# A gated attention and SwiGLU kernel: value fetches five attention steps later, four more places for transposed terms, and the output projection in float16 terms

## Chip, core and metric

One core of a Trainium2 chip runs the kernel. The core has five engines with instruction queues of their own: TensorE (PE; its weight loads are shown apart as PEld), VectorE (DVE), ScalarE (ACT), GpSimd (POOL) and SyncE (SP), which here issues every DMA. The metric is device microseconds of one execution; lower is better. The time before is the median of three runs.

## What is computed

The reference, cut to what matters (S = 2048 rows, D = 576, 32 heads of 18, 4 segments of 512 rows, F = 4608):

```python
def _A_ref(x, wq, wk, wv, wo, beta):              # attention with a memory
    q, k, v = heads(x @ wq), heads(x @ wk), heads(x @ wv)
    g = sigmoid(beta); M = 0; z = 0
    for s in range(4):
        p = softmax(qs @ ks.T * scale + mask)     # mask: -1e9 where key > query
        a_mem = (phi(qs) @ M) / (phi(qs) @ z + 1e-6)
        outs.append(g * a_mem + (1 - g) * (p @ vs))
        M = M + phi(ks).T @ vs; z = z + phi(ks).sum()
    return concat(outs) @ wo                      # the output projection

def _B_ref(x, w_gate, w_up, w_down):
    return (silu(x @ w_gate) * (x @ w_up)) @ w_down

g = sigmoid((x * gate_w).sum(-1, keepdims=True))
return g * _A_ref(x, ...) + (1 - g) * _B_ref(x, ...)
```

Inputs and outputs are float32. The kernel keeps the precision by splitting each operand of a matmul into a rounded high part and the low rest, and adding the products high x high, high x low and low x high.

## The kernel before

**Stages.** First come the projections to q, k and v and the memory term, segment by segment (`qk`, `v_step`, `upd_gen`, `mem_step`; to about 233 us). Their results go to DRAM: stacked bfloat16 terms of q and k (`stk`, `stw`), of v (`vd`), and the memory's part of the output (`med`). Then a loop over 72 positions works off the feed-forward part, with attention mixed in: `seq` has two halves of 1024 rows with 36 blocks of 128 hidden columns each. The first half also makes the float16 terms of the weights (`w_make`, kept in `wc` for the second half). Last comes the output projection over 16 tiles of 128 rows (`c_load`, `c_tr`, `products`).

**A position.** Gate and up projection of a block are made from seven products (`seven(t, j)`): six matmuls with 512 columns (line 1392) and one with the remainder rows of the weights, the tile `rh` (line 1395), which `r_fetch` loads from `rc` by line 356. After each product comes a beat (`tick`, `beat`), k = 0 to 7. In a beat run, in this order: the functions that were deferred to it (`defer`, a list of queues by beat); down projection groups, as many as `SHARE[k]` says; and steps of the attention. A down group (`down_part`, line 1161) is 9 matmuls of float16 terms into one PSUM bank, with 320 or 256 output columns, from three hidden blocks; DVE then adds the bank into `ya` (`down_end`, lines 1168 and 1170). Every third position 16 new groups are due. At position 3, the first with groups, another table `FSHARE` holds. Between the halves lies the break: ten beats without products, in which the last 16 groups of the first half run (two with `k` 0 and 1, the rest without a `k`).

**Attention.** `att_gen` is a generator, and each `next` is one step `tau`. Five steps make a unit of two heads in one segment (64 units). A step computes scores of the unit at hand (`s_bank`, line 890) for the row maxima. For most units the maximum row goes through DRAM (`m_store`, line 982; `row_load`, line 301) and the scores are computed again transposed twelve steps later (`t_bank`, line 1001), then exp on ACT (1005), a mask on POOL (1013), a split by DVE and POOL (1101, 1105) and the products with v (`pv_step`, 1029 and 1031). In the second half every other unit is turned instead: its exp is split into `pq` (946, 947), and a transposing DMA (`turn`, line 951) writes it to `pk`, from where `pv_turned` (963, 964) reads it. `homes` lists the places: six each for `pq` and `pk`. The table `TURN` says how many steps after the scores each part follows. `v_fetch` (line 306) loads the v terms of four units into one of two buffers. How many steps a beat runs comes from a credit that `TICK` fills; in the first half beats 0 and 1 give none, except in the break, where `brk` lets them.

**Order on the queues.** The schedule is manual: each engine executes its instructions in the order in which the program emits them, so a wait holds back all that follows on that engine. SP holds all DMA issues. In the first half ACT also squares raw weights for the scales of later blocks (`glance`: load by line 1371, square by line 141). `x_second` makes the terms of the second half's input from position 24 on, with low parts on DVE by line 1321.

**Output projection.** `wo_load` splits `wo` into float32r parts (1208, 1209). For each tile `c_tr` adds the memory's part, transposes through PE (1234, 1236), and splits into `oh`, `ol` and `os_` (133, 134). `products` (224) then runs 14 matmuls for each half of 288 columns, and DVE scales by the gate `gg` and adds the feed-forward part (1562, 1563).

## Time and profile before

| | |
|---|---|
| median of 3 runs | 1727.56 us (1726.11 to 1729.72) |
| the profiled execution | 1725.81 us, span 1724.1 us, mean granted clock 0.998 |
| projections and memory | 0 to 233 us |
| first half: positions 0 to 35 | 233 to 903 us |
| break | 903 to 926 us |
| second half: positions 36 to 71 | 926 to 1634 us |
| output projection (with the last down groups) | 1634 to 1724 us |
| busy: PE, DVE, ACT, POOL | 98%, 78%, 62%, 51% of the span |
| DMA | 311 MB, 61.8% of the 16 engines' time in the hardware queue |

How to read it: times count from the span's start. In a group or a timeline row stand line, engine, operation, output <- input with sizes, and in brackets the idle time before it with what ended it. A row of waits has the sum, the count and the longest. A row of the chain of waits has start and length on the path that ended last; matmuls of one run are merged there, so length over count is the pitch, while the duration of one matmul in other rows includes its way through the array. A row of a stretch has its limits, its length, and the busy time of PE, PEld, DVE, ACT and POOL, then the granted clock, DMA share and GB/s.

### The profile page before, as it was taken

The page shows a single profiled execution, that of the slowest core. Times are in us where ns is not written, and L with a number is a line of the kernel's source. Part 1 is how long each engine was busy: PE and PEld are TensorE (multiplying, and loading weights), DVE is VectorE, ACT ScalarE, POOL GpSimd, SP SyncE. Part 2 cuts the span into 40 slices and gives each one's busy share as a digit, 9 for nine tenths or more (in the row PEclk, how much of TensorE's full clock was granted, in tenths as well). Part 3 has the DMA queues.
Part 4 walks back from the last instruction along what each step waited for, and adds up shares of the span by engine and source line. Part 5 has one row for each costly group of instructions (what it writes and reads, how often), then busy time and mean ns, then how long its engine had stood idle before and what let it go on. Part 6 is the DMA issues. An engine that isn't in the chain of part 4 may idle for free.

```text
span 1724.1 us, 35228 instructions
## 1 busy us (share of the span) xinstructions
PE 1684.5 (98%) x12267; PEld 1093.1 (63%) x12267; DVE 1347.3 (78%) x3286; ACT 1066.3 (62%) x1907; POOL 885.6 (51%) x1187
## 2 busy tenths in 40 slices
PE   9999998999999999999999999999999999999999
PEld 7898865556655665565555556656656655665599
DVE  6687666789888988888886888887878787875555
ACT  6666567677777777766774664665565566464411
POOL 3336552266656665565553755555555555543121
PEclk9999999999999999999999999999999999999999
DMA  8666675665776666536435476786587669653543
GB/s 282 219 229 221 221 257 203 206 210 169 239 229 198 184 220 194 171 112 193 158 124 172 118 173 154 164 196 146 132 203 174 129 166 203 155 122 115 183 142 137
DMA packets 341670, 311.30 MB, mean 181 GB/s; under 512 B 193396, under 2 KB 258676, under 8 KB 341492
## 3 DMA queue, kind: packets, MB, share of 16 engines
q1 hardware_dynamic: 341492, 309.05, 61.8%
q8 instruction: 96, 1.57, 0.4%
q14 instruction: 82, 0.67, 0.1%
HBM read 183.20 MB, written 99.55 MB: 164 GB/s over the span
## 4 chain that ended last, share of the span: by engine, by line
PE 71%; DVE 10%; ACT 9%; issue 3%; DMA 3%; POOL 2%; SPq 1%; DVEq 0%; ACTq 0%; POOLq 0%
PE bank L1392 30%; PE bank L1161 19%; PE bank L224 7%; PE bank L1395 5%; PE bank L890 3%; PE bank L1001 2%; PE bank L1029 1%; ACT L1499 1%; DVE ya L1170 1%; ACT row L1499 1%; ACT pe L1005 1%; PE bank L1031 1%; PE bank L963 1%; DVE junk L908 1%; DMA stw<-q 1%
## 5 line engine op out<-in xcount | busy, mean ns | idle before, releaser
L1161 PE MATMUL bank<-dw,hh 128*128 128x320 f16 (+1 forms) x2304 | 437.9, 287 | 13.8 <-DVE ya L1170 9.5
L1161 PE MATMUL bank<-dw,hl 128*128 128x320 f16 (+1 forms) x1152 | 330.5, 287 | 0.9 <-DVE dw L1141 0.6
L1105 POOL TENSOR_TENSOR p<-pe,p 128x512 f16<-128x512 f32 x220 | 271.7, 1235 | 78.7 <-DVE p L1101 50.2
L1161 PEld LDWEIGHTS <-hh 128*128 128x128 f16 x2304 | 224.9, 98 | 100.9 <-issue 19.9
L1005 ACT ACTIVATE pe<-bank 128x512 f32<-128x512 f32 x220 | 130.1, 591 | 190.6 <-PE bank L1001 181.9
L1170 DVE SCALAR_TENSOR_TENSOR ya<-bank,sc,ya 128x320 f32<-128x320 f32 x352 | 177.2, 511 | 57.2 <-PE bank L1161 55.0
L1395 PE MATMUL bank<-xr,rh 128*128 128x512 f16 x504 | 191.2, 379 | 1.9 <-DMA rh<-rc 1.9
L908 DVE CUSTOM_DVE_ANT_0 junk<-bank,cm 128x128 bf16<-128x128 f32 (+2 forms) x352 | 169.3, 481 | 14.0 <-PE bank L890 7.4
L1013 POOL TENSOR_SCALAR_AFFINE_SELECT pe<-pe 128x256 f32<-128x256 f32 (+1 forms) x220 | 89.5, 407 | 164.6 <-ACT pe L1005 153.0
L1264 DVE SCALAR_TENSOR_TENSOR hl<-hh,row 128x512 f16<-128x512 f16 x144 | 125.2, 870 | 47.8 <-ACT hh L1261 46.7
L1161 PEld LDWEIGHTS <-hl 128*128 128x128 f16 x1152 | 112.7, 98 | 30.2 <-DVE hl L1264 0.6
L890 PE MATMUL bank<-kst,qst 108*128 108x512 bf16 (+3 forms) x512 | 124.8, 299 | 5.9 <-ACT pe L1005 5.2
L1001 PE MATMUL bank<-qst,kst 111*128 111x512 bf16 (+3 forms) x352 | 103.3, 300 | 3.9 <-ACT pe L1005 2.8
L1101 DVE CAST p<-pe 128x512 f16<-128x512 f32 x202 | 106.4, 527 | 0.0
L1497 DVE TENSOR_TENSOR row<-bank,row 128x512 f32<-128x512 f32 x72 | 49.7, 690 | 64.4 <-ACT bank L1496 64.4
L370 POOL TENSOR_TENSOR ws<-raw 128x256 f32<-128x256 f32 x72 | 66.5, 924 | 64.2 <-DMA raw<-in_wf_dram 35.3
L224 PE MATMUL bank<-xo,qhi 128*128 128x512 f32 x288 | 93.0, 403 | 0.5 <-DVE xo L134 0.2
L1261 ACT ACTIVATE hh<-row 128x512 f16<-128x512 f32 x144 | 89.0, 618 | 3.8 <-DVE row L1507 3.8
L467 POOL TENSOR_TENSOR q<-qr,q 128x512 bf16<-128x512 f32 x36 | 47.8, 1328 | 84.3 <-ACT q L466 74.8
L1492 ACT ACTIVATE row<-bank 128x512 f32<-128x512 f32 x72 | 42.9, 596 | 76.4 <-PE bank L1395 76.2
L1395 PEld LDWEIGHTS <-rh 128*128 128x128 f16 x504 | 49.3, 98 | 61.8 <-issue 2.4
L1496 ACT ACTIVATE bank<-bank 128x512 f32<-128x512 f32 x72 | 41.9, 582 | 72.6 <-PE bank L1395 70.7
(1090 smaller groups left out, 4228.3 us busy)
## 6 DMA issues: line engine op xcount, KB each, us to landing
xo<-in_wf_dram SPq DMA_DIRECT2D x65, 320.0 KB
raw<-in_wf_dram SPq DMA_DIRECT2D x72, 256.0 KB
dc<-dw SPq DMA_DIRECT2D x36, 432.0 KB
dw<-dc SPq DMA_DIRECT2D x36, 432.0 KB
rh<-rc SPq DMA_DIRECT2D x72, 168.0 KB
draw<-in_wd_dram SPq DMA_DIRECT2D x36, 288.0 KB
xo<-in_xT_dram SPq DMA_DIRECT2D x33, 256.0 KB
vd<-vps SPq DMA_DIRECT2D x8, 912.0 KB
```

What stands on the lines that cost most here:

```text
L224: nc.tensor.matmul(t, st[n], mv[n], start=(n == 0), stop=(n == 13))
L890: nc.tensor.matmul(t[:, c:c + w], qs[:KR, pr, P * i:P * i + P], ks[:KR, pr, 0:w], start=True, stop=True)
L908: nc.vector.tensor_tensor_reduce(junk.bitcast(BF)[:, :w], t[:, c:c + w], cm[:, L - w:L], 1.0, -3.0e38, OP.add, OP.max, m[:, k:k + 1])
L1001: nc.tensor.matmul(t[:, c:c + w], ks[:KR + 3, pr, P * j:P * j + P], qs[:KR + 3, pr, P * j:L], start=True, stop=True)
L1005: nc.scalar.activation(pe, t, AF.Exp, scale=SCALE)
L1101: nc.vector.tensor_copy(p1, pe)
L1105: nc.gpsimd.tensor_sub(p2, pe, p1)
L1161: nc.tensor.matmul(t, p, d[:, q, cs], start=(f == CH * c and n == 0), stop=(f == CH * c + CH - 1 and n == 2))
L1170: nc.vector.scalar_tensor_tensor(ya[:, i, cs], t, inv[c], ya[:, i, cs], op0=OP.mult, op1=OP.add)
L1264: nc.vector.scalar_tensor_tensor(lo, hi, -STEP, src, op0=OP.mult, op1=OP.add)
L1392: nc.tensor.matmul(t, w[:, p, z], x[z][:, q], start=first and n == 0, stop=False, skip_group_check=True)
L1395: nc.tensor.matmul(t, rem[:, RPOS[j]], XR[j], start=False, stop=True, skip_group_check=True)
```

## The change

The edits, with what each does:

- **Output projection.** `wo` and the attention output are split into float16 parts instead of float32r, with power-of-two scales. For these, twelve loads of `wo` and `wv` and twelve squares on ACT run in positions 41 to 60 (`o_scan`); at position 61 `o_scale` sums them over the partitions with one matmul and multiplies the scales' inverse into `gg`.
- **`rh`** gets a third buffer, and position 1's is fetched in the first stage (`n == 5` of the last segment's v steps) instead of in position 0.
- **Down groups of position 3** follow `SHARE`; `FSHARE` goes. **In the break** beats 0 and 1 run no attention step; `brk` goes.
- **Attention's loads.** `m_store` and `row_load` come one step later, the transposing DMA one step later (`TURN`), and `v_fetch` five steps later. `pk` gets four more places (`tp`).
- **`x_second`** moves some of its sums, high and low parts up to two beats ahead in its first position of each call.
- `reach` keeps the maximum in column 126 for `o_scale`.

```diff
-TURN = (1, 3, 7, 17)
+TURN = (1, 3, 8, 17)
-FSHARE = (0, 0, 0, 2, 3, 4, 4, 3)
...
-        nc.sync.dma_start(rhs[f % 2][:96].rearrange("p j n -> p (j n)"), rc[f // 4, :, f % 4])
+        nc.sync.dma_start(rhs[f % 3][:96].rearrange("p j n -> p (j n)"), rc[f // 4, :, f % 4])
...
-                    if n == 1:
-                        r_fetch(0)
+                    if n in (1, 5):
+                        r_fetch(n // 5)
...
+            homes["pk"] += [tp.tile([P, 8 * P], F16, name=f"pk{z}") for z in range(4)]
 
         def spot(name, u, n):
-            return homes[name][(5 * (u // 2) + n) % 6]
+            return homes[name][(5 * (u // 2) + n) % len(homes[name])]
...
-                if n == 1 and 1 <= u <= 2 * NB and u - 1 not in turned:
+                if n == 2 and 1 <= u <= 2 * NB and u - 1 not in turned:
                     m_store(u - 1)
-                if n == 3 and 1 <= u <= 2 * NB and u - 1 not in turned:
+                if n == 4 and 1 <= u <= 2 * NB and u - 1 not in turned:
                     row_load(u - 1)
...
-                z = tau - TL - VL - 1
+                z = tau - TL - VL - 6
                 if z % 20 == 0 and 0 <= z < N and z // 20 + 1 < 4 * NSEG:
                     v_fetch(z // 20 + 1)
...
-                wos.append(cps[0].tile([P, 2, NT, 288], F32R, name=f"wo{hf}", bufs=1))
+                wos.append(cps[0].tile([P, 2, NT, 288], F16, name=f"wo{hf}", bufs=1))
...
-            defer(n + 5, lambda: nc.scalar.activation(wos[hf][:, 0, :, c], box[0], AF.Copy))
-            defer(n + 7, lambda: nc.vector.tensor_sub(wos[hf][:, 1, :, c], box[0], f32(wos[hf][:, 0, :, c])))
+            k = column(12)
+            defer(n + 5, lambda: nc.scalar.activation(wos[hf][:, 0, :, c], box[0], AF.Copy, scale=k))
+            defer(n + 7, lambda: nc.vector.scalar_tensor_tensor(wos[hf][:, 1, :, c], box[0], k, wos[hf][:, 0, :, c],
+                                                                op0=OP.mult, op1=OP.subtract))
+
+        def o_scan(k):
+            w, c = divmod(k, 6)
+            src, c, box = (wo, wv)[w], slice(96 * c, 96 * c + 96), []
+
+            def load():
+                box.append(raw_tile()[:, :96 * NT])
+                nc.sync.dma_start(box[0].rearrange("p (k n) -> p k n", n=96), src[:, :, c])
+
+            return load, lambda: square(box[0], k, junk[:, :96 * NT])
+
+        def o_scale(k):
+            z = sc[:, 12:14]
+            if k == 0:
+                total(column(12), 0, 6)
+                total(column(13), 6, 12)
+            elif k == 1:
+                t = ts_tile([P, 2])
+                across(t, z)
+                nc.vector.tensor_scalar_max(z, t, FLOOR)
+                nc.gpsimd.tensor_scalar_mul(column(13), column(13), column(126))
+            elif k == 2:
+                grade(z, z)
+                nc.vector.tensor_scalar_mul(z, z, TOP)
+                nc.gpsimd.tensor_mul(column(14), column(12), column(13))
+            else:
+                nc.vector.reciprocal(column(14), column(14))
+                nc.gpsimd.tensor_scalar_mul(gg, gg, column(14))
...
-            oh = cps[0].tile([P, 4, P], F32R, name="oh")
-            ol = cps[0].tile([P, 4, P], F32R, name="ol")
-            os_ = cps[0].tile([P, P], F32R, name="os")
-            split(oh, ol, ta)
-            xs_split(os_, tb)
+            oh = cps[0].tile([P, 4, P], F16, name="oh")
+            ol = cps[0].tile([P, 4, P], F16, name="ol")
+            os_ = cps[0].tile([P, P], F16, name="os")
+            k = column(13)
+            split_16(oh, ol, ta, k)
+            nc.scalar.activation(os_, tb, AF.Copy, scale=k)
+            nc.vector.scalar_tensor_tensor(os_[64:128], tb[64:128], k[64:128], os_[64:128], op0=OP.mult, op1=OP.subtract)
...
-            share = (SHARE, FSHARE)[early[0]][k]
+            share = SHARE[k]
...
-                credit[0] += TICK[half][busy] * (opened[0] if half else k > 1 or brk[0])
+                credit[0] += TICK[half][busy] * (opened[0] if half else k > 1)
...
-                steps += ((0, 3, high, 0), (0, 4, low, 0), (0, 5, total, 1), (0, 5, high, 5), (0, 6, low, 5), (0, 7, total, 4),
+                steps += ((0, 3, high, 0), (0, 4, low, 0), (0, 4, total, 1), (0, 4, high, 5), (0, 5, low, 5), (0, 5, total, 4),
...
-                steps += ((0, 5, high, 0), (0, 6, low, 0), (0, 7, total, 1), (1, 2, high, 5), (1, 3, low, 5), (1, 4, total, 4),
+                steps += ((0, 4, high, 0), (0, 5, low, 0), (0, 5, total, 1), (1, 2, high, 5), (1, 3, low, 5), (1, 4, total, 4),
...
-                plan.append((1 if nxt[1] else 10, lambda f=nxt[1]: r_fetch(f)))
+                if pos:
+                    plan.append((1 if nxt[1] else 10, lambda f=nxt[1]: r_fetch(f)))
...
+            if FT + 6 <= pos + 1 < FT + 24 and pos % 3 == 2:
+                pair = [o_scan((pos + 1 - FT - 6) // 3 * 2 + k) for k in range(2)]
+                plan += [(2 + 3 * k, z[0]) for k, z in enumerate(pair)]
+            if FT + 6 <= pos < FT + 24 and pos % 3 == 0:
+                plan += [((1, 7)[k], z[1]) for k, z in enumerate(pair)]
+            if pos == FT + 25:
+                plan += [((1, 4, 6, 8)[k], lambda k=k: o_scale(k)) for k in range(4)]
```

Lines behind line 40 have other numbers in the changed kernel: 1161 is 1162 there, 1168 is 1169, 224 is 223, 1395 is 1429. Three places where the order moves:

VectorE at position 3, where the first drains of down groups (`ya<-bank`) stand; `row<-bank` of the last row but one is line 1497. Before:

```order
L1489 TENSOR_TENSOR bank_3163<-bank_3113,row 128x512
L1264 SCALAR_TENSOR_TENSOR hl<-hh,row 128x512
L1381 RECIPROCAL gg<-gg 128x16
L378 SCALAR_TENSOR_TENSOR wo__3147<-raw,sc,wo__3147 128x256
L1382 TENSOR_SCALAR g_82<-gg 128x16
L1168 TENSOR_SCALAR ya<-bank_3193,sc 128x320
L908 ISA junk,mb_2438<-bank_3204,cm 128x512
L908 ISA mb_2438 128x1
L1168 TENSOR_SCALAR ya<-bank_3207,sc 128x256
L1497 TENSOR_TENSOR row<-bank_3113,row 128x512
L1168 TENSOR_SCALAR ya<-bank_3237,sc 128x320
```

and now:

```order
L1415 RECIPROCAL gg<-gg 128x16
L1169 TENSOR_SCALAR ya<-bank_3181,sc 128x320
L1169 TENSOR_SCALAR ya<-bank_3192,sc 128x256
L377 SCALAR_TENSOR_TENSOR wo__3152<-raw,sc,wo__3152 128x256
L1416 TENSOR_SCALAR g_82<-gg 128x16
L1169 TENSOR_SCALAR ya<-bank_3220,sc 128x320
L907 ISA junk,mb_2438<-bank_3231,cm 128x512
L907 ISA mb_2438 128x1
L1169 TENSOR_SCALAR ya<-bank_3234,sc 128x256
L1538 TENSOR_TENSOR row<-bank_3118,row 128x512
L1169 TENSOR_SCALAR ya<-bank_3264,sc 128x320
```

Four drains instead of two stand ahead of the sum `row<-bank` (1497, now 1538).

TensorE at the start of the break, up to the first down group. Before, with the end of the second attention step:

```order
L1001 LDWEIGHTS kst_2766
L1001 MATMUL bank_11941<-qst_2768,kst_2766 128x128
L890 LDWEIGHTS qst_2767
L890 MATMUL bank_11943<-kst_2765,qst_2767 128x512
L1001 LDWEIGHTS kst_2766
L1001 MATMUL bank_11941<-qst_2768,kst_2766 128x384
L1161 LDWEIGHTS hh
L1161 MATMUL bank_11958<-dw,hh 128x320
```

and now:

```order
L1426 LDWEIGHTS wo__11804
L1426 MATMUL bank_11842<-xo_2484,wo__11804 128x512
L1429 LDWEIGHTS rh_2446
L1429 MATMUL bank_11842<-xr_1756,rh_2446 128x512
L1162 LDWEIGHTS hh
L1162 MATMUL bank_11884<-dw,hh 128x320
```

The down groups follow the last product of position 35 directly; two attention steps between them are gone.

TensorE at the first matmuls of the output projection (`oh`, `ol` are the transposed attention output's parts, `wo_` the weights'). Before:

```order
L1161 LDWEIGHTS hl
L1161 MATMUL bank_22336<-dw,hl 128x256
L224 MATMUL bank_22347<-wo_21944,oh 128x288
L224 MATMUL bank_22347<-wo_21944,ol 128x288
L224 MATMUL bank_22347<-wo_21944,oh 128x288 x2
```

and now:

```order
L1162 LDWEIGHTS hl
L1162 MATMUL bank_22394<-dw,hl 128x256
L223 LDWEIGHTS oh
L223 MATMUL bank_22405<-wo_22026,oh 128x288
L223 LDWEIGHTS ol
L223 MATMUL bank_22405<-wo_22026,ol 128x288
```

The number of matmuls is the same; the weight loads, which the program had left inside the float32r matmuls, are instructions of their own.

More of the change, by code (lines that the diff above doesn't have):

```diff
@@ L795, in gated_mix @@
                 wraw_of[0] = [w_load(0, u) for u in range(2)]
-                for z in range(2):
+                for z in range(3):
                     rhs.append(wop.tile([P, 7, P], F16, name=f"rh{z}", bufs=1))
@@ L827, in gated_mix @@
                         first_split(6, n)
-                    for k, t, v in ((0, rhs[0][96:], 0.0), (1, kst[0], -1.0), (3, kst[1], -1.0), (6, rhs[1][96:], 0.0)):
+                    for k, t, v in ((0, rhs[0][96:], 0.0), (1, kst[0], -1.0), (3, kst[1], -1.0), (4, rhs[1][96:], 0.0)):
                         if n == k:
                             nc.gpsimd.memset(t, v)
-                    if n == 1:
-                        r_fetch(0)
+                    if n in (1, 5):
+                        r_fetch(n // 5)
                     if n > 2:
@@ L921, in gated_mix @@
         turned = set()
+        tp = pool(st, "tp", 1)
         def turn_open(u):
@@ L1254, in gated_mix @@
         credit = [-1.0]
-        opened, early, brk = [0], [0], [0]
+        opened = [0]
         later = [False]
@@ L1468, in gated_mix @@
             later[0] = half == 1 and f > 0
-            early[0] = int(pos == CH)
             turn_of[0] = () if pos < 24 else (1, 3)
-            ops, rem = wops.pop((half, f)), rhs[f % 2]
+            ops, rem = wops.pop((half, f)), rhs[f % 3]
             hh = fp.tile([P, 2, L], F16, name="hh")
```

6 lines of the change are left out of this document (3 added, 3 removed).

## The prediction

> **What bounds the kernel now.** I read the busy shares first, then the stretches, then what TensorE (PE) waited for, and last the timeline around its longest waits.
>
> ```profile
> PE 1684.5 (98%) x12267; PEld 1093.1 (63%) x12267; DVE 1347.3 (78%) x3286; ACT 1066.3 (62%) x1907; POOL 885.6 (51%) x1187
> ```
>
> PE is busy for 98% of the span, so only two things can help: less PE work, or fewer PE waits. The stretches (length, then busy time of PE, PEld, DVE, ACT, POOL, then granted clock, DMA share, GB/s) show where PE has gaps:
>
> ```profile
> 233.00:269.00 36.00, 33.62 (x158) 15.01 (x157) 21.80 (x40) 27.85 (x50) 14.72 (x23) 1.00 0.60 207
> 269.00:297.00 28.00, 23.02 (x139) 14.00 (x138) 17.50 (x50) 21.86 (x45) 5.12 (x9) 0.94 0.83 289
> 297.00:903.00 606.00, 594.88 (x4186) 351.79 (x4186) 521.68 (x1204) 441.00 (x796) 353.24 (x494) 1.00 0.60 186
> 903.00:926.00 23.00, 20.32 (x149) 15.30 (x149) 17.51 (x38) 7.73 (x12) 8.53 (x8) 0.93 0.44 158
> 926.00:1634.00 708.00, 700.02 (x5679) 420.07 (x5678) 545.00 (x1466) 406.39 (x677) 375.93 (x495) 1.00 0.65 159
> 1634.00:1724.00 90.00, 86.30 (x672) 81.73 (x669) 52.15 (x101) 13.40 (x34) 17.16 (x24) 0.99 0.42 142
> ```
>
> Two short stretches stand out: 5.0 us of 28 idle from 269 on, and 2.7 of 23 at the break between the halves (903 on). In both the clock is under 1. The long second half (926 on) has only 8.0 us of gaps in 708. So the change can gain in the short stretches and in the output stage, and hardly in the second half, where most of its edited lines act.
>
> **The change, part by part.** Base of the sum: the profiled execution's 1725.8 us (span 1724.1), 1.7 below the median of the runs shown, 1727.6.
>
> *Output projection in fp16.* The chain of waits has pure runs of back-to-back matmuls:
>
> ```profile
> 1592.78 2.21 PE bank L1161 x18
> 1666.26 3.72 PE bank L224 x28
> ```
>
> The first is fp16: nine of 320 and nine of 256 columns, 288 on the mean, one every 2.21/18 = 122.8 ns. The second is the projection, 288 columns in fp32r, one every 3.72/28 = 132.9 ns. There are 16 tiles x 2 halves x 14 = 448 of them: 448 x 10.1 ns = **4.5 us** off PE. Bounds: 0, if the pitch stays, and 4.5; I take 4.5, since the fp16 row has the same columns and a new stationary tile for each matmul as well. The splits behind it keep their number; DVE is busy 52 and ACT 13 of the last 90 us, which hides them.
>
> *What feeds the scale.* Twelve loads of 240 KB and twelve squares on ACT are new, in positions 41 to 60 of 72, and at position 61 some dozen tiny operations with one matmul of two columns.
>
> ```profile
> L1115 ACT ACTIVATE junk<-draw 128x576 f16<-128x576 f32 x36 | 24.2, 673 | 0.0
> ```
>
> At the 0.67 us of this similar square that is 8 us of ACT, idle for 302 of the 708 us; the loads are 2.9 MB beside 113 (159 GB/s x 708 us). Each square comes seven beats or more after its load. Cost 0, with that cover; for the matmul of two columns, which waits for sums made three beats before, 0.3 us. Without the cover, rival 3.
>
> *First remainder fetch earlier.* rh for position 1 is now fetched one stage earlier, into one of three buffers.
>
> ```profile
> 242.83 0.43 SPq L356 DMA_DIRECT2D rh<-rc  x1
> 247.59 0.38 PE L1395 MATMUL bank<-xr,rh 128*128 128x512 f16 x1 [1.93 <-DMA rh<-rc]
> 252.53 0.60 ACT L1492 ACTIVATE row<-bank 128x512 f32<-128x512 f32 x1 [1.51 <-PE bank L1395]
> 253.00 0.72 POOL L370 TENSOR_TENSOR ws<-raw 128x256 f32<-128x256 f32 x1 [7.34 <-DMA raw<-in_wf_dram]
> ```
>
> The wait of 1.93 goes. What is late next is the weight load for position 2: it lands at 253.0, just when ACT wanted it. With ACT 1.9 us earlier it waits there instead, and passes most of that on to the bank copy behind it. Gain between 0.4 and 1.9; I take **1.2**.
>
> *Down groups of position 3.* `FSHARE` goes, so the first two of 16 down groups run one beat earlier, before product 3 instead of behind it.
>
> ```profile
> 275.04 0.81 DVE L1139 SCALAR_TENSOR_TENSOR dw<-draw,sc,dw 128x576 f16<-128x576 f32 x1
> 276.43 0.31 DVE L1141 TENSOR_SCALAR dw<-dw 128x576 f16<-128x576 f16 x1
> 276.79 0.30 PE L1161 MATMUL bank<-dw,hl 128*128 128x320 f16 x1 [0.59 <-DVE dw L1141]
> 281.98 0.38 PE L1161 MATMUL bank<-dw,hh 128*128 128x256 f16 x2 [0.74 <-DVE ya L1168]
> 283.38 0.74 ACT L141 ACTIVATE xo<-xo 128x640 f32<-128x640 f32 x1 [1.97 <-DMA xo<-in_wf_dram]
> 284.73 0.69 DVE L1497 TENSOR_TENSOR row<-bank,row 128x512 f32<-128x512 f32 x1 [2.80 <-ACT bank L1496]
> 285.33 0.54 DVE L1168 TENSOR_SCALAR ya<-bank,sc 128x320 f32<-128x320 f32 x1
> 285.93 0.69 PE L1161 MATMUL bank<-dw,hh 128*128 128x320 f16 x2 [2.80 <-DVE ya L1168]
> ```
>
> Now: an ACT square waits for its load until 283.38, the bank copy L1496 stands behind it, DVE's L1497 behind that, and behind L1497 the drain that PE's fifth group needs. After: the first group starts at 273.2 and still can't end before 276.8 (L1141), so PE idles some 2.4 us there, with group 2 and product 3 queued behind, and ACT's copy of product 3 (279.6 anyway, behind two squares) waits for that; from 276.8 on it does group 2 (1.0), product 3 (1.5), groups 3 and 4 with an attention bank (2.4) and product 4 (1.5), to about 283.6. Drains 3 and 4 now stand ahead of L1497, so group 5 can start at once, where it started at 285.93: 2.3 us, less 0.3 for group 7, which still stands behind L1497. **2.0**; bounds 0 (all of the new idle is added) and 4.1 (none).
>
> Right behind that gap the clock is low:
>
> ```profile
> 286.00:288.00 2.00, 2.00 (x8) 1.06 (x8) 0.88 (x3) 1.98 (x3) 0.00 (x0) 0.50 1.05 392
> 288.00:290.00 2.00, 2.00 (x9) 0.98 (x8) 1.32 (x5) 0.74 (x2) 0.00 (x0) 0.69 0.79 297
> ```
>
> That costs 2 x 0.50 + 2 x 0.31 = 1.6 us. The two gaps of 2.8 us are followed by it, the gaps up to 1.93 are not; the new idle of 2.4, broken by two matmuls, lies between. I take **1.0** of 1.6.
>
> *Break.* Two attention steps at the end of the first half go; the attention loop ends two steps later. The rows are from the timeline, the 144 from the chain of waits, the last from the stretches:
>
> ```profile
> 901.25 0.33 PE L1001 MATMUL bank<-qst,kst 111*128 111x384 bf16 x1
> 903.09 0.63 ACT L1261 ACTIVATE hh<-row 128x512 f16<-128x512 f32 x1 [1.55 <-DVE row L1507]
> 903.85 0.69 DVE L1264 SCALAR_TENSOR_TENSOR hl<-hh,row 128x512 f16<-128x512 f16 x1
> 905.68 0.22 PE L1001 MATMUL bank<-qst,kst 111*128 111x128 bf16 x1 [2.79 <-ACT pe L1005]
> 906.43 19.31 PE bank L1161 x144
> 907.00:909.00 2.00, 2.00 (x11) 1.33 (x10) 1.75 (x4) 1.20 (x3) 1.96 (x3) 0.51 1.01 341
> ```
>
> 144 matmuls at 122.8 ns are 17.7; they took 19.3, again 1.6 behind a gap. After: the groups start at 901.25, do 12 matmuls of older blocks (to 902.7), wait for hh (903.7) and hl (904.5), and end 130 matmuls later at 920.5 instead of 925.7. From those 5.2 go the two steps' matmuls, which PE does later (1.6 + 0.8 = 2.4): **2.8**. Bounds: 4.4 (no new wait) and 1.2 (low clock all the same).
>
> *Second-half input splits.* Two DVE splits (L1321) move a beat ahead in positions 24 and 30.
>
> ```profile
> 683.92 0.74 DVE L1321 SCALAR_TENSOR_TENSOR xo<-xo,sc 128x512 f16<-128x512 f32 x1
> 696.83 1.65 DVE L1321 SCALAR_TENSOR_TENSOR xo<-xo,sc 128x512 f16<-128x512 f32 x1
> 698.99 0.43 PE L1161 MATMUL bank<-dw,hh 128*128 128x320 f16 x2 [1.58 <-DVE ya L1170]
> 815.23 0.43 PE L1161 MATMUL bank<-dw,hh 128*128 128x320 f16 x2 [1.58 <-DVE ya L1170]
> ```
>
> In both places a slow split delays a drain that PE waits for. One beat earlier DVE also has drains to do, so I keep 0.6 of each wait: 2 x 1.0 = **2.0**; bounds 3.2 and -1.
>
> *Value fetches, stores, transposes, places.* SP runs in order, and these stood in its way:
>
> ```profile
> SPq L306 <- PE bank L890: 84.2, 9, 13.5
> SPq L951 <- PE bank L964: 33.5, 10, 7.6
> ```
>
> A value fetch five steps later no longer waits for the buffer's last reader, and transposes into ten places instead of six don't wait for the last unit's products. The maximum row's store and load come a step later, ahead of a use three steps on. That frees SP, but in the second half PE has 8.0 us of gaps in all, mostly from DVE and ACT. **0.5**; bounds 4 and -4, the latter since every step after the break shifts by two against the products and may meet other work on DVE.
>
> Sum: 4.5 + 1.2 + 2.0 + 1.0 + 2.8 + 2.0 + 0.5 - 0.3 = 13.7. On the median: **1713.9 us**.
>
> [...]
>
> **Rivals.** (1) *The front gives its gains back.* ACT is busy 27.9 of 36 and 21.9 of 28 us before 297, and the DMA share is 0.83: positions 1 to 3 may be paced by ACT and the loads. Then output and break remain, perhaps half of the splits: 7.3 + 1 = 8.3, 1719. Chance 0.18. (2) *SP was worth more.* Half of the second half's gaps go (4), and all of the low clock and both split waits: 13.7 + 3.5 + 0.6 + 1.2 = 19, 1708.5. 0.12. (3) *Slower: the scans block ACT.* A square in ACT's order whose load is late does what L141 does at 283.38: 2.8 us of PE and 1.6 of clock, 4.4 each. From four of twelve on (17.6) the change loses; at six, 1740. For it: such loads waited 1.97 there. Against it: DMA share 1.0 there, 0.65 here, and seven beats (17 us) of lead. 0.07. (4) *Low clock not tied to the gaps* (1.6 + 1.0 stay): 1716.5. 0.05. (5) *fp16 keeps the pitch*, so the projection does not do what it says: 1718.4. 0.05.
>
> **How the numbers follow.** Forecast 0.53, rivals 0.18, 0.12, 0.07, 0.05, 0.05. A difference under 0.2% (3.5 us) can't be told from none here. Slower by more: rival 3, 0.07; within it: the weak end of rival 1, 0.05; faster: the rest, 0.88. The forecast's own range is 1709 to 1719; taking in rival 1 and most of rival 2 the range is 1706 to 1722.
>
> **What would show it.** Right: projection runs of 28 near 3.44 us; no PE wait at rh in position 1; a PE wait near 2.4 us ahead of the first down group and none of 2.8 at the fifth; the break's 144 matmuls directly behind the last product with a wait under 2 us and clock 1.00; L1321 waits under 1 us. Wrong: ACT waiting for raw loads of wo or wv in the second half, PE gaps there well over 8 us, or the first weights' load ending PE's wait at position 2.

## The result, and the profile after

| | before | changed |
|---|---|---|
| median of the runs beside the forecast | 1729.72 us (1726.11 to 1732.30, 5 runs) | 1719.04 us (1716.62 to 1720.42, 5 runs) |
| ratio, beside the forecast | | 0.9940 (95% interval 0.9928 to 0.9953) |
| median, third series of the experiments | 1727.35 us (9 runs) | 1718.72 us (5 runs) |
| ratio, third series | | 0.9948 (0.9936 to 0.9961) |
| span of the profiled execution | 1724.1 us | 1717.1 us |

The change makes the kernel faster by 8.6 to 10.7 us; 13.7 were forecast, 1713.9 us with a range of 1706 to 1722. The likeliest value was too good by some 4 us. Where they are missing is the question of what follows.

First the busy shares of the changed kernel, then its stretches (length, busy time of PE, PEld, DVE, ACT, POOL, granted clock, DMA share, GB/s), cut where its own break and output stage begin:

```profile
PE 1679.5 (98%) x12269; PEld 1077.8 (63%) x12269; DVE 1353.8 (79%) x3295; ACT 1076.6 (63%) x1930; POOL 889.2 (52%) x1191
```

```profile
233.00:269.00 36.00, 34.44 (x162) 15.61 (x161) 23.36 (x44) 27.90 (x50) 15.21 (x23) 1.00 0.61 212
269.00:297.00 28.00, 24.97 (x156) 15.58 (x155) 18.44 (x53) 21.95 (x45) 4.46 (x9) 0.94 0.82 289
297.00:901.00 604.00, 593.78 (x4136) 349.54 (x4135) 521.51 (x1202) 441.29 (x797) 355.96 (x495) 1.00 0.60 186
901.00:922.00 21.00, 18.54 (x135) 13.93 (x136) 15.17 (x24) 5.63 (x9) 4.54 (x4) 0.92 0.50 172
922.00:1632.00 710.00, 701.65 (x5733) 422.75 (x5732) 549.67 (x1489) 415.45 (x703) 378.58 (x501) 1.00 0.68 162
```

PE's idle time in the two front stretches falls from 2.4 and 5.0 to 1.6 and 3.0 us, and in the first half from 11.1 to 10.2. In the break it is 2.5 instead of 2.7, with the clock at 0.92 instead of 0.93: nothing was won there. In the second half it is 8.4 instead of 8.0. PE's busy time falls by 5.0 us, and that is the output projection, by the chain of waits of the changed kernel:

```profile
1663.25 3.43 PE bank L223 x28
```

28 matmuls take 3.43 us where they took 3.72. From the first to the last of the 448 the trace has 73.4 us, before 78.3: **4.9 us** (forecast 4.5).

PE's timeline of the changed kernel in the front (start, length, what ran, and in brackets the wait ahead of it and what ended it):

```profile
248.53 1.46 PE L1426 MATMUL bank<-xo,wo__2849 128*128 128x512 f16 x6 [0.53 <-ACT bank L1519]
...
274.25 0.31 PE L1162 MATMUL bank<-dw,hh 128*128 128x320 f16 x1 [0.23 <-ACT hh L1295]
275.70 0.30 PE L1162 MATMUL bank<-dw,hh 128*128 128x320 f16 x1 [1.14 <-DVE dw L1140]
276.59 0.30 PE L1162 MATMUL bank<-dw,hl 128*128 128x320 f16 x1 [0.59 <-DVE dw L1142]
...
297.52 0.43 PE L1162 MATMUL bank<-dw,hh 128*128 128x320 f16 x2 [0.96 <-DVE ya L1169]
```

The wait for rh in position 1 is gone, and a bank copy has 0.53 us of it. At position 3 PE waits 0.23 + 1.14 + 0.59 = 1.96 us ahead of and within the first down group, and not 2.80 at the fifth. This is as forecast (2.4 and none). The break is not. PE there, then what DVE and POOL did in the same microseconds:

```profile
901.39 0.45 PE L1162 MATMUL bank<-dw,hh 128*128 128x320 f16 x2 [0.89 <-ACT hh L1295]
903.90 0.31 PE L1162 MATMUL bank<-dw,hl 128*128 128x320 f16 x1 [2.06 <-DVE hl L1298]
```

```profile
899.93 0.74 DVE L1548 SCALAR_TENSOR_TENSOR row<-bank,sc,row 128x512 f32<-128x512 f32 x1
900.59 1.36 DVE L1549 SCALAR_TENSOR_TENSOR row<-row,sc 128x512 f32<-128x512 f32 x1
901.88 1.37 DVE L1142 TENSOR_SCALAR dw<-dw 128x576 f16<-128x576 f16 x1
903.17 1.28 DVE L1298 SCALAR_TENSOR_TENSOR hl<-hh,row 128x512 f16<-128x512 f16 x2
```

```profile
900.14 2.94 POOL L1381 TENSOR_TENSOR raw<-raw 128x512 f32<-128x512 f32 x2 [14.30 <-DVE dw L1140]
```

The attention steps are gone from the break, yet PE waits 0.89 + 2.06 = 2.95 us where it waited 2.79. DVE's second gate product (1549) takes 1.36 us and the third term of dw (1142) 1.37; before the change the same two (1508 and 1141 there) took 0.74 and 0.30. Both run while POOL subtracts input remainders (1381). L1548, which reads a PSUM bank and began before them, keeps its 0.74. Before the change POOL worked on the attention's masks and splits from 905.70 on, and its subtractions (1347 there) came at 910.10, behind the splits that PE waited for:

```profile
902.98 0.74 DVE L1508 SCALAR_TENSOR_TENSOR row<-row,sc 128x512 f32<-128x512 f32 x1
903.63 0.30 DVE L1141 TENSOR_SCALAR dw<-dw 128x576 f16<-128x576 f16 x1
```

```profile
905.70 0.41 POOL L1013 TENSOR_SCALAR_AFFINE_SELECT pe<-pe 128x256 f32<-128x256 f32 x1 [17.48 <-ACT pe L1005]
910.10 2.61 POOL L1347 TENSOR_TENSOR raw<-raw 128x512 f32<-128x512 f32 x2
```

The low clock stayed too. Windows of 3.41 us of the changed kernel, two pairs:

```profile
273.59:277.00 3.41, 1.46 (x10) 0.65 (x8) 2.77 (x6) 2.67 (x7) 0.00 (x0) 1.00 0.89 318
277.00:280.42 3.42, 3.42 (x13) 1.70 (x12) 2.54 (x7) 1.23 (x3) 1.45 (x2) 0.50 1.03 392
...
901.64:905.06 3.42, 1.35 (x12) 0.90 (x11) 3.42 (x6) 2.47 (x4) 1.44 (x1) 1.00 0.27 101
905.06:908.47 3.41, 3.41 (x17) 2.26 (x15) 0.99 (x3) 0.00 (x0) 0.00 (x0) 0.50 0.97 292
```

A granted clock of 0.50 for 3.41 us each time: 1.7 us twice, as before.

The split waits in positions 24 and 30: PE's waits from 675 to 825 us (in all, how often, the longest), of the kernel before and then of the changed one:

```profile
PE bank L1161 <- DVE ya L1170: 4.3, 4, 1.6
PE bank L890 <- ACT pe L1005: 1.6, 2, 0.8
PE bank L1031 <- POOL p L1105: 0.2, 1, 0.2
```

```profile
PE bank L1162 <- DVE ya L1171: 2.4, 4, 1.0
PE bank L1032 <- POOL p L1106: 0.8, 2, 0.4
```

6.1 us became 3.2.

### The profile page after: what moved, and what is told of

The parts are those of the page before. It is cut to its first block, busy times and chain, and to the rows that moved or that the text cites. A ratio compares the mean times of both kernels' runs of the same rounds, so it can differ in the third digit from the quotient of the medians.

```text
span 1717.1 us, 35318 instructions
## 1 busy us (share of the span) xinstructions
PE 1679.5 (98%) x12269; PEld 1077.8 (63%) x12269; DVE 1353.8 (79%) x3295; ACT 1076.6 (63%) x1930; POOL 889.2 (52%) x1191
## 4 chain that ended last, share of the span: by engine, by line
PE 73%; DVE 12%; ACT 7%; issue 3%; DMA 3%; POOL 1%; SPq 1%; DVEq 0%; ACTq 0%; POOLq 0%
PE bank L1426 31%; PE bank L1162 18%; PE bank L223 8%; PE bank L1429 5%; PE bank L889 3%; PE bank L1002 2%; DVE ya L1171 1%; PE bank L1030 1%; ACT L1540 1%; DVE junk L907 1%; PE bank L1032 1%; PE bank L964 1%; DVE p L1102 1%; ACT row L1540 1%; DMA rc<-rt 1%
## 5 line engine op out<-in xcount | busy, mean ns | idle before, releaser
L1106 POOL TENSOR_TENSOR p<-pe,p 128x512 f16<-128x512 f32 x220 | 271.9, 1236 | 75.3 <-DVE p L1102 50.6
L907 DVE CUSTOM_DVE_ANT_0 junk<-bank,cm 128x128 bf16<-128x128 f32 (+2 forms) x352 | 169.3, 481 | 13.7 <-PE bank L889 7.3
L1298 DVE SCALAR_TENSOR_TENSOR hl<-hh,row 128x512 f16<-128x512 f16 x144 | 129.7, 902 | 45.7 <-ACT hh L1295 44.8
```

Source lines behind the costliest of these rows:

```text
L907: nc.vector.tensor_tensor_reduce(junk.bitcast(BF)[:, :w], t[:, c:c + w], cm[:, L - w:L], 1.0, -3.0e38, OP.add, OP.max, m[:, k:k + 1])
L1106: nc.gpsimd.tensor_sub(p2, pe, p1)
L1298: nc.vector.scalar_tensor_tensor(lo, hi, -STEP, src, op0=OP.mult, op1=OP.add)
```

## The experiments

They ran in three series, each beside runs of the kernel before on the same chip. The series differ (medians of the kernel before: 1728.67, 1725.94 and 1727.35 us), so ratios are compared: 0.001 is 1.7 us, the changed kernel is at 0.9940 and 0.9948, and with half widths of 0.0010 to 0.0014 a difference under some 3 us between two kernels is not settled by the ratios; the rows must tell. The kernel before also had a higher mean granted clock in the second series (0.9982, against 0.9975 and 0.9976), which by 0.001 for 1.7 us is worth some 1.1 us. So the ratios of that series may stand up to 0.0006 too high beside the changed kernel's, which come from other series; whether they do is not shown.

**The output in fp32r again** (first series).

```diff
-wos.append(cps[0].tile([P, 2, NT, 288], F16, name=f"wo{hf}", bufs=1))
+wos.append(cps[0].tile([P, 2, NT, 288], F32R, name=f"wo{hf}", bufs=1))
-oh = cps[0].tile([P, 4, P], F16, name="oh")
+oh = cps[0].tile([P, 4, P], F32R, name="oh")
```

`ol` and `os_` likewise, and the splits write fp32r.

> The changed kernel with the output projection's terms (wo and the transposed rows) kept in fp32r; the scale, its scans and everything else stay. Theory (the fp16 terms save PE time by their pitch): runs of 28 projection matmuls go back from about 3.5 to 3.72 us, the stretch from the first to the last of the 448 from 73.4 to about 78.3 us, and the run is 4.5 to 5 us longer than the changed kernel. Rival (the pitch is set by something else in this stage, such as the weight loads or the splits): the stretch stays at 73.4 and the time within 1 us of the changed kernel.

Measured: 1724.18 us, ratio 0.9974 (0.9965 to 0.9984), 4.5 to 5.9 us longer than the changed kernel; the chain of waits has the old runs, and the 448 matmuls take 78.3 us again:

```profile
1666.94 3.72 PE bank L223 x28
```

With the type of the terms the pitch changes, 132.9 ns in fp32r and 122.5 in fp16; whether by the matmul itself or by its weight load, which takes 188 ns in fp32r and 98 in fp16, is not separated. It is about half of the whole gain.

**FSHARE back at position 3** (first series). Edit: `share = (SHARE, FSHARE)[early[0]][k]` with `early[0] = int(pos == CH)`, as before the change.

> The changed kernel with FSHARE back at position 3, so the first down group runs a beat later again. Theory (the earlier groups only trade one gap for another and the clock drops behind either): PE waits about 2.8 us ahead of the fifth group again, no 1.1 and 0.6 us ahead of the first ones, granted clock 0.5 for some 3.4 us behind it either way; the run is 0.5 to 1.5 us longer than the changed kernel. Rival (the terms as forecast, 2.0 for the groups and 1.0 for the clock): 3 us longer. Rival (nothing won there): 0 to 0.5 us.

Measured: 1720.67 us, 0.9952 (0.9939 to 0.9965), 0.7 to 2.1 us longer. PE's timeline has the late waits again (1163 is 1162 here, 1170 is 1169):

```profile
284.01 0.38 PE L1163 MATMUL bank<-dw,hh 128*128 128x256 f16 x2 [2.49 <-DVE ya L1170]
286.88 0.69 PE L1163 MATMUL bank<-dw,hh 128*128 128x320 f16 x2 [1.72 <-DVE ya L1170]
```

PE's waits from 265 to 300 us add up to 5.8 us, against 3.5 in the first profile of the changed kernel and 4.0 in its second, and 5.0 before the change. The groups' term is thus 1.0 to 1.5 us as the change found it. A low clock for one window followed here as well.

**The attention steps back in the break** (first series). Edit: the credit again counts `k > 1 or brk[0]`, with `brk[0] = 1` ahead of the break's beats.

> The changed kernel with the attention steps of the break put back (credit also in its first beats). Theory (the break's gain was given back: without those steps GpSimd subtracts the input remainders while VectorE makes the splits that PE waits for): the gap ahead of the break's groups is about 2.8 us as before the change, the subtractions run behind the attention's work again, VectorE's dw third goes back from 1.37 to 0.30 us, and the time is within 1 us of the changed kernel. Rival (as forecast, the steps cost 2.8 us there): 2.8 us longer.

Measured: 1721.04 us, 0.9962 (0.9950 to 0.9975), 2.4 to 3.8 us longer. PE and POOL in the break:

```profile
901.86 0.22 PE L1002 MATMUL bank<-qst,kst 111*128 111x128 bf16 x1 [2.79 <-ACT pe L1006]
```

```profile
906.27 2.61 POOL L1381 TENSOR_TENSOR raw<-raw 128x512 f32<-128x512 f32 x2
```

In the break the theory holds: the wait is 2.79 us as before the change, POOL's subtractions come behind the attention's work, and the dw third takes 0.30 us. The time does not: it fits the rival (2.8 us), though without the rival's reason. In the profile the loss lies behind the break, where PE is idle for 11.5 of the 710 us from 922 on (8.4 in the changed kernel), with waits for a stack load (1.8 us) and a weight load (0.9) that the changed kernel does not have. So taking the steps out may have been worth about what was forecast, but behind the break and not in it. With the steps in the break the kernel before had only 8.0 us of idle time there, so this hangs on the other edits as well. One profile does not settle that part.

**POOL held behind hl** (first series).

```diff
+if pos == 35:
+    plan.append((11, lambda: nc.gpsimd.tensor_copy(column(127), hl[:, 0, 0:1])))
     plan += [(o, fn) for o, fn in third if o >= 0]
```

> The changed kernel with one GpSimd copy of a single column of hl ahead of the four remainder subtractions in the break, so they cannot start before VectorE has written hl. Theory (the subtractions slow VectorE, and the long gap brings the low clock): VectorE's second gate product takes 0.74 instead of 1.36 us and the dw third 0.30 instead of 1.37, hl is there 1.5 to 1.7 us earlier, PE's wait for it falls from 2.06 to about 0.5 us, no granted clock of 0.5 follows; the run is 3 to 3.5 us shorter than the changed kernel. Rival A (the clock drop has another cause): the wait falls, the clock of 0.5 stays, 1.5 to 1.7 us shorter. Rival B (VectorE is slow there for another reason): no change of VectorE's durations, 0.

Measured: 1714.35 us (1713.04 to 1714.59), 0.9916 (0.9903 to 0.9929), 4.1 to 5.5 us shorter. DVE (1550 is 1549 here), POOL and PE in the break:

```profile
898.65 0.74 DVE L1550 SCALAR_TENSOR_TENSOR row<-row,sc 128x512 f32<-128x512 f32 x1
899.31 0.31 DVE L1142 TENSOR_SCALAR dw<-dw 128x576 f16<-128x576 f16 x1
```

```profile
900.83 2.62 POOL L1381 TENSOR_TENSOR raw<-raw 128x512 f32<-128x512 f32 x2
```

```profile
900.27 0.31 PE L1162 MATMUL bank<-dw,hl 128*128 128x320 f16 x1 [0.37 <-DVE hl L1298]
```

With POOL's subtractions 2.6 us later, counted from the first down group, and nothing else moved, both DVE operations have their old lengths, and PE's wait for hl is 0.37 instead of 2.06 us. Rivals A and B fall: what was to be won in the break had gone to POOL's subtractions. All five runs had a mean granted clock of 1.000, and the time is better than the 3 to 3.5 us expected. Part of that is chance: the low window at position 3, which lies ahead of this edit, is absent as well, while it came in four of the ten profiles that keep the changed kernel's order there (on the mean 0.4 windows of 1.7 us, some 0.7 us). Why DVE is slower beside POOL is not shown; measured are 1.36 and 1.37 us beside the subtractions and 0.74 and 0.31 without them.

**Four groups' older blocks first** (second series).

```diff
-down_groups(2 if len(groups) == 16 else 1, wide_tile)
-if groups and len(groups) < 14:
+down_groups(4 if len(groups) == 16 else 1, wide_tile)
+if groups and len(groups) < 12:
```

> The changed kernel with the break's older blocks of four down groups instead of two ahead of the wait for the last position's hh and hl: 12 matmuls more, 1.48 us, run inside the gap. Theory (the granted clock drops for one window of 3.41 us when PE was busy for less than some 0.43 of the window ahead of it, windows lying on a fixed grid): the gap falls from 2.95 to about 1.5 us, which is too short to leave a window under 0.43, so the clock stays at 1.00 in the break; 1.5 us from the gap and 1.7 from the clock where the changed kernel had it, 1.5 to 3.2 in all. Rival A (the clock drops behind any idle time here): 1.5, with the clock of 0.5 still behind it. Rival B (banks 0 and 2 are not free yet): no change.

Measured: 1715.17 us, 0.9937 (0.9925 to 0.9949), 0.5 to 1.9 us shorter by the ratios.

```profile
902.17 0.31 PE L1162 MATMUL bank<-dw,hl 128*128 128x320 f16 x1 [1.72 <-DVE hl L1298]
```

The gap falls from 2.95 to 1.72 us, no low clock follows it, and the runs' clock is 0.9995 on the mean (0.9988 in ten runs of the changed kernel). The rows fit the theory; the time is at the low end of the 1.5 to 3.2 us expected or below it.

**The changed kernel once more** (third series, no edit).

> The changed kernel once more, unedited, as the mark for the others of this series on one chip. Theory (the clock's windows lie on a grid that has another phase in each execution): ratio to the kernel before between 0.993 and 0.995, and the granted clock of 0.5 behind the gaps at position 3 and in the break in some executions and not in others, each time for 3.41 us and behind a window in which PE was busy for less than about 0.45. Rival (the drops belong to the gaps): both drops again at the same places.

Measured: 1718.72 us, 0.9948. Windows of 3.41 us on this execution's grid:

```profile
271.87:275.28 3.41, 2.04 (x12) 0.98 (x11) 1.58 (x3) 3.40 (x9) 0.00 (x0) 1.00 0.99 315
275.28:278.70 3.42, 2.83 (x19) 1.67 (x18) 3.42 (x9) 1.29 (x5) 1.78 (x2) 1.00 1.05 378
```

```profile
899.92:903.34 3.42, 0.64 (x4) 0.27 (x5) 3.42 (x4) 2.63 (x5) 2.32 (x2) 1.00 0.00 0
903.34:906.75 3.41, 3.41 (x16) 2.01 (x15) 1.49 (x4) 0.36 (x1) 0.00 (x0) 0.50 0.98 333
```

The same three waits at position 3 (0.23, 1.14 and 0.59 us) were followed by the low clock in the first profile and not in this one, because here the border between two windows (275.28) lies among them: 2.04 and 2.83 us of PE in the two, where the other execution had 1.46 in one. In the break the drop came in both.

**The third down block's split a beat earlier** (third series).

```diff
-defer(2, lambda: nc.vector.scalar_tensor_tensor(d[:, 1], r, k, d[:, 0], op0=OP.mult, op1=OP.subtract))
+defer(1 if f == CH - 1 else 2, lambda: nc.vector.scalar_tensor_tensor(d[:, 1], r, k, d[:, 0], op0=OP.mult, op1=OP.subtract))
-o, third = 3, lambda: nc.vector.tensor_scalar_mul(d[:, 2], d[:, 0], 1.0 / STEP)
+o, third = 2 if f == CH - 1 else 3, lambda: nc.vector.tensor_scalar_mul(d[:, 2], d[:, 0], 1.0 / STEP)
```

> The changed kernel with VectorE's split of the third down block (and the third term behind it) one beat earlier, so that it stands ahead of the split of hl for which VectorE waits 2.78 us with this split ready behind it. Theory (the first down group of position 3 waits for an order on VectorE, not for work): PE's waits of 1.14 and 0.59 us there fall to about 0.4 in all, no clock of 0.5 can follow, and the run is 1 to 3 us shorter than the changed kernel. Rival (what stands behind takes it back: the fifth group waits for the drain behind the bank sum that ScalarE's late square holds up): the waits fall, but PE waits 1 us or more at the fifth group, and the run is 0 to 1 us shorter.

Measured: 1718.03 us, 0.9951 (0.9938 to 0.9965), the same as the changed kernel beside it.

```profile
275.06 0.30 PE L1162 MATMUL bank<-dw,hl 128*128 128x320 f16 x1 [0.50 <-DVE dw L1142]
...
285.23 0.43 PE L1162 MATMUL bank<-dw,hh 128*128 128x320 f16 x2 [0.66 <-DVE ya L1169]
```

The waits at the first group fall from 1.96 to 0.73 us, and the rival is nearly right about the rest (it had 1 us or more at the fifth group): two drains now cost 0.20 and 0.66 us (none and 0.43 in the changed kernel beside it). From 265 to 300 us PE waits 3.2 us instead of 4.0. Position 3 is held by several late things in a row.

**The three edits together** (third series): POOL held behind hl, four groups first, the split a beat earlier.

> The changed kernel with the three edits together: the subtractions held behind hl in the break, four groups' older blocks first there, the third block's split a beat earlier at position 3. Theory: the break's gap falls from 2.95 to about 0.2 us and position 3's from 2.4 to about 0.9, with no clock of 0.5 in either place: 2.7 and 1 to 1.5 us from the gaps and up to 1.7 each from the clock, 4 to 7 us shorter than the changed kernel, 0.990 to 0.991 of the kernel before. Rival (the gains do not add, since the loads then pace the front and the second half's start): 2 to 4 us.

Measured: 1712.98 us (1711.03 to 1713.79), 0.9915 (0.9901 to 0.9928), 5.7 us shorter than the changed kernel beside it and 14.4 shorter than the kernel before. From 890 to 912 us, around the break, PE is busy for 21.56 of 22.00 us. The clock was 1.000 in all four runs. By the ratios it is not better than POOL held alone (0.9916).

**Attention loads and places as before** (second series). Edit: `TURN[2]` 7, six places for `pk`, the maximum row's store and load at `n == 1` and `n == 3`, the value fetch at `tau - TL - VL - 1`.

> The changed kernel with the attention's loads and places as before: value fetches five steps earlier, the maximum row's store and load a step earlier, transposes after 7 instead of 8 and into six places for pk. Theory (they free SP, which PE hardly waits for): SP is blocked some 80 us at the value fetch again, PE's idle time from 930 to 1630 us stays within 1 us of the changed kernel's, and so does the run. Rival A (SP was worth more): 3 to 4 us longer. Rival B (the shifted steps cost the new gaps of about 1 us at 997, 1243 and 1278): 1 to 2 us shorter.

Measured: 1716.61 us, 0.9948 (0.9934 to 0.9962), the same to 1.4 us longer. SP's longest waits, of the changed kernel and then of this one:

```profile
SPq L1151 <- PE bank L1162: 62.3, 9, 11.3
```

```profile
SPq L305 <- PE bank L889: 66.7, 8, 14.4
```

SP is blocked at the value fetch again, and without that it is blocked at another load instead: freeing SP mostly moved its wait. Neither rival is seen; the gaps near 997 and 1243 us remain, and one new wait of 2.55 us for a stack load near 1269 us stands in this profile.

**The splits at their old beats** (second series). Edit: in `x_second`, (0, 5, total, 1), (0, 6, low, 5) and their neighbours instead of one or two beats earlier.

> The changed kernel with the second half's input splits at their old beats in positions 24 and 30. Theory (a split that stands ahead of a drain on VectorE makes PE wait): the waits of 1.6 us behind the drains near 697 and 813 us return and PE loses 2 to 3 us more between 675 and 825 us; the run is 2 to 3 us longer. Rival (VectorE gives it back elsewhere): those waits return, but others between 675 and 825 us go, and the time stays within 1 us.

Measured: 1721.52 us, 0.9973 (0.9963 to 0.9982), 4.3 to 5.7 us longer. PE's waits from 675 to 825 us are 5.4 + 1.6 + 0.4 = 7.4 us (3.2 in the changed kernel). A slow split and POOL at the same time:

```profile
696.46 1.65 DVE L1355 SCALAR_TENSOR_TENSOR xo<-xo,sc 128x512 f16<-128x512 f32 x1
```

```profile
696.03 1.53 POOL L1106 TENSOR_TENSOR p<-pe,p 128x512 f16<-128x512 f32 x1 [1.34 <-PE bank L889]
```

The rival falls. The loss is larger than the 2 to 3 us expected, and near the 4.2 us of waits that came back. The split that takes 1.65 us instead of 0.75 meets POOL as in the break.

**The remainder's fetch as before** (second series). Edit: two buffers, `r_fetch(1)` in the plan of position 0.

> The changed kernel with two remainder buffers and the remainder of position 1 fetched where it was. Theory (PE's wait of about 2 us for rh in position 1 returns, and part of it is covered by the weights' wait behind it): PE's idle time from 233 to 265 us grows by 1.2 to 1.6 us, and so does the run. Rival A (all of it is covered): 0 to 0.4. Rival B (it also takes down groups and clock at position 3 along): 3 us.

Measured: 1719.11 us, 0.9961 (0.9947 to 0.9975), 2.2 to 3.6 us longer.

```profile
247.07 0.38 PE L1428 MATMUL bank<-xr,rh 128*128 128x512 f16 x1 [1.30 <-DMA rh<-rc]
```

PE waits for rh again, 1.30 us this time. But its waits from 233 to 265 us grow by only 0.6 us, from 1.4 to 2.0, and not by the 1.2 to 1.6 expected, since those for the bank copies fall from 1.1 to 0.4. The time lost is more than the rows show and does not decide between the theory and rival B.

**Without the scans** (third series): the twelve loads and squares are left out.

> The changed kernel without the twelve loads and twelve squares that feed the projection's scale (left out; the scale is then made from stale sums). Theory (they are hidden by idle ScalarE and DMA time): within 1 us of the changed kernel, and PE's idle time from 930 to 1630 us within 1 us of it. Rival (the squares or loads block ScalarE's order in the second half): 2 us or more shorter, with the gaps near 997, 1034, 1096 and 1243 us gone.

Measured: 1718.84 us, 0.9950 (0.9936 to 0.9964), as the changed kernel (1718.72). The squares cost ACT 7.1 us, and PE nothing that shows: from 930 to 1630 us it is idle for 8.3 us here and for 8.4 in the changed kernel beside it.

```profile
L140 ACT ACTIVATE junk<-raw 128x480 f16<-128x480 f32 x12 | 7.1, 592 | 2.7 <-DVE mb L907 2.7
```

That is the group of ACT in the changed kernel, with 2.7 us of idle time before it that VectorE ended, not a load.

## Why the prediction was off by 4 us

| term | forecast, us | shown, us | by what |
|---|---|---|---|
| output in fp16 | 4.5 | 4.9 | matmul stretch 78.3 to 73.4, fp32r run |
| remainder fetch | 1.2 | 0.9 | PE's waits 233 to 265 us, 2.3 to 1.4 |
| groups of position 3 | 2.0 | 1.0 to 1.5 | PE's waits 265 to 300 us, FSHARE run |
| clock behind them | 1.0 | 0 or 1.7 | two profiles of one kernel |
| break | 2.8 | -0.2 | 2.79 to 2.95 us of wait, clock as before; more behind the break by the run with the steps back |
| second-half splits | 2.0 | 2.9 | PE's waits 675 to 825 us, 6.1 to 3.2 |
| fetches, places | 0.5 | about 0 | run with them undone |
| scale | -0.3 | 0 | run without the scans |

Most sizes shown are those of rows. The runs that take one edit back give others, by the middles of their ratios 5.2 us for the output, 2.9 for the fetch, 1.4 for the groups, 3.1 for the break, 5.0 for the splits and 0.7 for the fetches and places. That is 18 us for a change worth 8.6 to 10.7. How much of the excess is noise and how much comes from edits that hang on each other is not shown.

- **Break: the step that failed.** The prediction let PE "wait for hh (903.7) and hl (904.5)", taking DVE's and ACT's times as they stood. It moved the attention steps away and counted only what PE did in them. It did not ask what POOL, which they had kept busy, would do earlier: its subtractions came forward by some 8 us, counted from the last product, onto DVE's splits, and 0.62 + 1.07 = 1.7 us more on DVE went straight into PE's wait. The run with POOL held shows it: PE's wait for hl falls from 2.06 to 0.37 us. It also makes the forecast's break nearly true: 0.89 + 0.37 us of wait and no low clock.
- **Clock: right that it follows the gaps, wrong about how.** The prediction sorted gaps by length (2.8 yes, 1.93 no, 2.4 in between). The profiles show fixed windows of 3.41 us, and a gap that may lie in one of them or across two. As a mean over runs the term can be read from the granted clocks: 0.9978 in 37 runs of the kernel before on three chips, 0.9988 in ten of the changed one, 0.0010 or 1.7 us; 1.0 and the break's 1.6 had been forecast.
- **Position 3: mechanism right, half the size.** The first group waits for L1140 and L1142 and the fifth no longer for the bank sum, as said; a drain costs 0.96 us at 297.52 now. The prediction's own steps (276.8 + 1.0 + 1.5 + 2.4 + 1.5) add up to 283.2 where it says about 283.6; by them its term would have been 2.4, further off.
- **Output and splits: right**; the splits' term was 0.9 too small, since an attention wait of 0.8 us at either place went as well (the row of 1.6 us for L890). What the prediction did not see is why the splits were slow: they ran beside a POOL operation on two tensors (L1106 for 1.53 us at 696.03 in the run with the old beats), and moved ahead they take 0.75 us (at 689.70 and 805.04) instead of 1.65.
- **Second half: right that it would not move.** 84 us of SP's waits at the value fetch went, and PE's idle time there is 8.4 instead of 8.0.
- **The rivals.** The first gave about the time that was measured (1719), but not for its reason: the front kept about half of its gain without the clock's share, nearly all with it, and the break kept none. The third (scans block ACT) and the fifth (fp16 keeps the pitch) are excluded by the runs. The fourth, a low clock not tied to the gaps, does not hold as it stands: each low window follows one with idle time, but at position 3 its coming depends on the grid as well. The result lies at the upper edge of the forecast's own range (1709 to 1719). That it lies well inside the full range is in part luck, since that reached up to 1722 for the sake of the first rival, whose reason did not come true.

Without the clock the terms shown add up to 9.8 us (with 1.25 for position 3); new waits between 300 and 675 us take 0.9 of them (3.8 to 4.7) and the second half 0.4, which leaves 8.5. The profiled spans, with two low windows in each, differ by only 7.0. The times of PE's products, from the first to the last of each stage, show where the 1.5 between are (us):

| | before | changed | changed once more |
|---|---|---|---|
| up to the first product of position 0 | 233.1 | 233.5 | 233.1 |
| first half, products | 668.3 | 665.5 | 665.0 |
| break | 24.2 | 22.5 | 22.6 |
| second half, products | 708.3 | 709.8 | 710.0 |
| output stage | 90.2 | 85.8 | 85.8 |
| low windows within | 2 | 2 | 1 |

The break is 1.7 us shorter and the second half 1.5 longer: the two steps' matmuls moved, and little else. The output stage gave 4.4 and not 4.9, and the first half 2.8 and not the some 4.2 that its waits give (0.9 + 1.25 + 2.9 - 0.9). What PE lost there beside the waits that the rows list stays open. With the clock's mean of 1.7 the 7.0 make 8.7, the low end of the 8.6 to 10.7 measured.

## What to carry to other kernels

When work leaves a stage, list what every engine in that stage will now do earlier, and whether the engine that the critical wait hangs on is slower beside it: here POOL ran ahead, two DVE operations beside it took 1.7 us longer, and PE waited 2.95 us where it had waited 2.79. A one-column copy that makes the helper wait for the critical result was worth 4.1 to 5.5 us, more than most edits of this change. And when a profile shows a clock drop behind a gap, look at several executions before pricing it: either make the gap shorter (of 1.72 us, in the run with four groups first, it drew no low clock), or fill it with work that is ready.

## What the runs showed of the hardware

**The low clock came in whole windows of 3.41 us, on a grid whose phase differed between executions.** Every low stretch within the program lasted 3.413 us in the profiles of the kernel before and the changed one, and the distance between the two in each is a whole multiple of it (before: 621.2 us from 285.81 to 907.04, 182 windows; changed: 628.1 us from 277.00 to 905.06, 184). Two executions of the changed kernel had the grid at 273.59 and at 271.87 us. Windows of the kernel before, the first not followed by a drop:

```profile
244.85:248.26 3.41, 1.48 (x8) 0.54 (x7) 2.02 (x3) 2.76 (x5) 0.81 (x3) 1.00 0.99 303
```

```profile
903.62:907.04 3.42, 1.36 (x9) 0.80 (x9) 3.21 (x14) 3.07 (x6) 0.41 (x1) 1.00 0.65 213
907.04:910.45 3.41, 3.41 (x17) 2.21 (x16) 2.61 (x6) 1.16 (x3) 3.41 (x4) 0.50 0.71 238
```

Around the gaps of the front, of the break and, in one run, near 1269 us, all eleven windows of this case's profiles with PE busy for 0.51 to 1.36 us, and so idle for at least 2.05, were followed by one at half clock; of six with 1.42 to 1.59 us, three were; none with 1.66 or more was. The run with the steps back has a wait of 2.79 us and no drop, since it fell across two windows:

```profile
897.03:900.45 3.42, 2.03 (x47) 1.62 (x46) 2.70 (x5) 1.85 (x4) 0.00 (x0) 1.00 0.30 105
900.45:903.86 3.41, 2.00 (x15) 1.35 (x15) 3.20 (x13) 3.08 (x6) 1.05 (x2) 1.00 0.69 230
```

This is part of the spread between runs of one kernel: of the 14 runs of the kernel before on one chip, in the second series, the two at a clock of 0.996 took 1729.9 us on the mean, the seven at 0.998 took 1726.3 and the two at 1.000 took 1723.4.

**VectorE's slow operations here all met GpSimd.** 0.30 to 1.37 us for a single-input fp16 scaling, 0.74 to 1.36 and 0.75 to 1.65 for two others, each beside a POOL operation on two tensors; L1548, with one operand in PSUM, had 0.74 although POOL started in the middle of it. In the traces of the kernel before and the changed one 184 and 188 VectorE instructions took over 30% longer than the quick ones of the same line and shape (their lower quartile; groups of at least four, of 0.25 us or more each), and every one of the 372 overlapped a GpSimd instruction; of the 3833 others in these groups 2342 overlapped one and stayed quick.
